# Where the block sums of the last batch's first weight matrix are made: group 1 early and by way of DRAM, group 0 at an earlier place in the plan

## The chip, the cores and the metric

The kernel runs as one program on one core of a Trainium2 chip. The metric is device time in microseconds (us). Before the change the median of three runs is 398.04 us (397.66 to 398.58). Profiles show one execution with the start and end of every instruction: PE is TensorE (PEld its weight loads), DVE is VectorE, ACT ScalarE, POOL GpSimd, SP the engine whose queue issues most DMAs.

## The reference, cut to what matters

```
for t in range(S):                                   # S = 768, 4 batches, 8 heads of 48
    cur   = einsum('bhd,bhe->bhde', u * k[t], v[t])
    y[t]  = einsum('bhd,bhde->bhe', r[t], state + cur)
    state = w * state + einsum('bhd,bhe->bhde', k[t], v[t])
x  = y.transpose(0, 2, 1, 3).reshape(B, S, 384)
u_ = x + (x^T @ U @ V)^T                             # mixes along the sequence, rank 32
out = u_ + relu(u_ @ w_ch1) @ w_ch2                  # 384 -> 1536 -> 384
```

All is float32; the kernel keeps that precision by splitting operands into a high and a low part and multiplying hi*hi, lo*hi and hi*lo.

## The kernel before, in words

Work goes batch by batch (four of them). Attention of a batch runs in six chunks of 128 steps, merged into the MLP of the batch before, so that TensorE always has matrix products of the MLP to go on with. At the end of a batch's attention `c_g` (L1214) sums x with U on TensorE, `c_u` (L1237) adds the low-rank mix to x, and for batches 2 and 3 `c_store`, `c_blocks` and `c_turn` (L1296 to L1325) carry the result through DRAM and turn it into the transposed operands `uTh` and `uTl`.

The MLP's first layer multiplies by W1 (12 column blocks, each held as `w1s`, hi and lo), the second by W2 (`w2s`). For batches 0 to 2 it is plain (`m_1`, `m_2`). In the last batch the first layer takes three column blocks at a time (a group, `NG` = 4 of them) and forms their 18 block products from 15 products of sums (`fifteen`, L1411): sums of blocks of u (`u_sums`, L1347, 11 of them, needed once) and sums of blocks of W1 (`w_sums`, L1380, 9 for each group). For one group `w_sums` issues three additions hi + lo of whole W1 blocks (L1388), 15 additions or subtractions of 128 x 128 blocks into a tile `ws` (L1400), and for each of three sets of three sums a copy on ACT to the hi part `wh` (L1404) and a subtraction to the lo part `wl` (L1405). L1388, L1400 and L1405 may go to either DVE or POOL.

In `fifteen` each product is three matmuls into a PSUM bank (names c and a letter in the profile; group 0 also borrows the banks tr and sc). The copies `keep` (L1432), the differences `less` (L1436), and in `out` the final additions (L1441, L1443), the relu to `hh` (L1445, ACT) and the low part `hl` (L1447, DVE) follow. The chains D and A use the ring of two banks tagged "mm", as do G, H and so on in the groups after the first. A new chain can start in a bank only when the last `out` that reads it is done.

The order of all instructions is written out by a list scheduler in the kernel, `Plan` (L48): each operation gets a key, the time at which it is wanted (`at`, L1717), and a guess of its duration. An engine takes the operation that can start first, and among those that can start at the same time the one of the lowest key. An operation that can go to POOL or DVE is marked as using the two engines' shared port ("lock"), and the plan never runs two of these at once. Tiles with a tag come from a ring of so many buffers and are handed out strictly in the order of the keys. The order on each engine is then fixed; on the chip each engine runs its list in order and waits for semaphores.

The keys that matter here are in us of the plan: the last batch's MLP begins at t = 315.95, its attention ends at `end` = 270.3. `w_sums(0)` has the key t - 20 = 295.95, groups 1, 2 and 3 have 313.35, 333.7 and 354.05. Rings: "xl" (4 buffers) holds `gf`, `ut` and later x5, x4 and one `hl`; "xh" (4) the blocks that come back from DRAM (`ub`), the raw sums of u and x3 to x0; "kT" (2) attention's transposed k and then `ws`; "ldr", "ldk", "ks" (2 each, called `W_TAGS` after) attention's loads and then `wh` and `wl` of one set; "dv" (2) attention's dv, then the third hi + lo sum `wr` of a group and the low part of the sum u20. The other two hi + lo sums are kept in the tiles `ub` and `tab` (attention's own, free after its last chunk).

The lines around the change:

```
US, WS, A3 = (16.0, 2.5), (20.0, 10.0), (0, 7.5)
...
for g in range(NG):
    at(t - WS[g > 0] + (7.4 + 20.35 * (g - 1) if g else 0), lambda g=g: w_sums(g))
for i, (f, m) in enumerate(last_units()):
    at(t - FIRST3[i] * PER if i < 3 else t, f)
    t += m * PER / 3 if i > 2 else 0
```

Of the kernel before, what the change touches and what calls it, by code (L numbers as in the profile page):

```python
# [9 lines left out]
F32 = mybir.dt.float32  # L10
# [314 lines left out]
def rwkv_moe(ctx: ExitStack, tc: tile.TileContext, r, k, v, w, u, U, V, w1, w2, out):  # L325
# [38 lines left out]
    def wbuf(shape, dt, tag, bufs, name):  # L364
        return Buf(work, shape, dt, tag, bufs, name)
# [14 lines left out]
    def f32(ap):  # L380
        return ap.bitcast(F32)
# [12 lines left out]
    def on_dve(n, fn, w_, r_, port=False, dk=0.0):  # L394
        return op("DVE", dve(n), lambda: fn(nc.vector), w_, r_, lock=port, dk=dk)

    def on_act(n, fn, w_, r_, times=1, dk=0.0):
        return op("ACT", times * (act(n) - 94) + 94, fn, w_, r_, dk=dk)

    def on_either(n, fn, w_, r_, dk=0.0, only=None):  # L400

        ways = [("POOL", pool(n), lambda: fn(nc.gpsimd), True), ("DVE", dve(n), lambda: fn(nc.vector), True)]
        return one_of(ways, w_, r_, only, dk)
# [907 lines left out]
    def c_turn(b, t, ct):  # L1311
# [10 lines left out]
        if last and (ct, t) in ((1, 1), (2, 0)):  # L1322
# [22 lines left out]
    NG = NFT // 3  # L1345

    def u_sums():  # L1347

# [28 lines left out]
                    ops_u[ct, t] = ([(lambda uh=uh, ct=ct: uh.t[:, ct, :]), (lambda ul=ul, ct=ct: ul.t[:, ct, :])], [(uh, ct), (ul, ct)])  # L1377
        return [lambda a_=a_: one(*a_) for a_ in U_SUMS] + [plain]

    def w_sums(g):  # L1380

        f0 = 3 * g
        raw = [(lambda: ub.t.rearrange("p h d -> p (h d)"), ub), (lambda: tab.t, tab)]
        third = wbuf([128, DM], F32, "dv", 2, f"wr_{g}")
        raw.append((lambda: third.t, third))
        for i, (ap, buf) in enumerate(raw):
            wt = W1[f0 + i]
            on_either(384, lambda e, ap=ap, wt=wt: e.tensor_tensor(ap(), f32(wt.t[:, 0]), f32(wt.t[:, 1]), ALU.add), [buf], [wt])  # L1388
        for s, tag in enumerate(("ldr", "ldk", "ks")):
            hi, lo = (wbuf([128, 3, 128], F32R, tag, 2, f"w{'hl'[k]}_{g}_{s}") for k in range(2))  # L1390
            sm = wbuf([128, 3, 128], F32, "kT", 2, f"ws_{g}_{s}")
            for j, (n, blocks, signs) in enumerate(W_SUMS[3 * s:3 * s + 3]):
                def block(x):
                    i, c = x
                    return (lambda: raw[i][0]()[:, c * 128:(c + 1) * 128]), raw[i][1]
                (acc, rb) = block(blocks[0])
                rd = [rb]
                for x, sg in zip(blocks[1:], signs):
                    fb, rb = block(x)
                    on_either(128, lambda e, acc=acc, fb=fb, sg=sg, sm=sm, j=j: e.tensor_tensor(  # L1400
                        sm.t[:, j], acc(), fb(), ALU.add if sg > 0 else ALU.subtract), [(sm, j)], rd + [rb])
                    acc, rd = (lambda sm=sm, j=j: sm.t[:, j]), []
                ops_w[g, n] = ([(lambda hi=hi, j=j: hi.t[:, j]), (lambda lo=lo, j=j: lo.t[:, j])], [hi, lo])
            on_act(384, lambda hi=hi, sm=sm: nc.scalar.copy(hi.t, sm.t), [hi], [sm])  # L1404
            on_either(384, lambda e, hi=hi, lo=lo, sm=sm: e.tensor_tensor(lo.t, sm.t, f32(hi.t), ALU.subtract), [lo], [hi, sm])  # L1405
        for i in range(3):
            wt = W1[f0 + i]
            for c in range(NCT):
                ops_w[g, (i, c)] = ([(lambda k=k, wt=wt, c=c: wt.t[:, k, c * 128:(c + 1) * 128]) for k in range(2)], [wt])

    def fifteen(g):  # L1411

        b, f0 = B - 1, 3 * g
        banks, kept = {}, {}
        early = {"G": "tr", "I": "sc", "K": "av", "H": "tr", "J": "sc"} if g == 0 else {}
        homes = {"x5": ("xl", NXS), "x4": ("xl", NXS), "x3": ("xh", NXS), "x2": ("xh", NXS), "x1": ("xh", NXS), "x0": ("xh", NXS)}

        def product(chain, w_, u_, first=False, last=False):
            if first:
                banks[chain] = bank(early.get(chain, "mm"), f"c{chain}_{g}")  # L1420
            pt = banks[chain]
            (wf, wb), (uf, ub_) = ops_w[g, w_], ops_u[u_]

            def go():
                for j, (kw, ku) in enumerate(((0, 0), (1, 0), (0, 1))):
                    whole(pt.t[:, :TB], lhsT=wf[kw](), rhs=uf[ku](), start=first and j == 0, stop=j == 2, skip_group_check=True)
            pe(3 * MM, go, [pt], wb + ub_)

        def keep(name, chain):
            pt = banks[chain]  # L1430
            to = kept[name] = wbuf([128, TB], F32, *homes.get(name, ("ldv", 3)), f"{name}_{g}")
            on_act(384, lambda: nc.scalar.copy(to.t, pt.t[:, :TB]), [to], [pt])  # L1432

        def less(name, a_, b_, o_=ALU.subtract):
            to, x, y = kept[name], kept[a_], kept[b_]
            on_either(384, lambda e: e.tensor_tensor(to.t, x.t, y.t, o_), [to], [v_ for v_ in (x, y) if v_ is not to])  # L1436

        def out(name, chain, t, i, minus=False):
            x, pt = kept[name], banks[chain]
            if minus:  # L1440
                on_dve(384, lambda e: e.tensor_tensor(x.t, x.t, pt.t[:, :TB], ALU.subtract), [x], [pt])  # L1441
            else:
                on_dve(384, lambda e: e.tensor_tensor(x.t, pt.t[:, :TB], x.t, ALU.add), [x], [pt])  # L1443
            hh = xbuf([128, TB], F32R, *(("x", NX) if i == 0 else ("hh", NH)), f"hh_{b}_{t}_{f0 + i}")
            on_act(384, lambda: nc.scalar.activation(hh.t, x.t, AF.Relu), [hh], [x])  # L1445
            hl = wbuf([128, TB], F32R, "xl", NXS, f"hl_{b}_{t}_{f0 + i}") if i == 0 else xbuf([128, TB], F32R, "hl", NH, f"hl_{b}_{t}_{f0 + i}")
            on_dve(384, lambda e: e.scalar_tensor_tensor(hl.t, x.t, 0.0, f32(hh.t), ALU.max, ALU.subtract), [hl], [x, hh])  # L1447
            hs[b, t, f0 + i] = (hh, hl)

        def s_G():  # L1450
            product("G", (0, 0), "u51", True)
            keep("x1", "G")

        def s_s32():
            product("G", "w193", (0, 1))
            keep("x5", "G")

        def s_H():
            product("H", (0, 1), "u40", True)
            keep("h", "H")  # L1460
            less("x1", "h", "x1")

        def s_I():
            product("I", (1, 0), "u15", True)
            keep("x2", "I")

        def s_s16():
            product("I", "w328", (0, 0))
            keep("x4", "I")

        def s_K():
            product("K", "w34", "u36", True)
            keep("x0", "K")

        def s_s8():
            product("K", "w26", "u12")
            keep("x3", "K")

        def s_J():
            less("x3", "x3", "h", ALU.add)  # L1480
            product("J", (1, 2), "u20", True)
            keep("j", "J")
            less("x2", "j", "x2")
            less("x0", "j", "x0")

        def s_D():
            product("D", (2, 1), "u10", True)
            keep("d", "D")
            less("x5", "x5", "d")

        def s_A():
            product("A", (2, 2), "u17", True)
            keep("a", "A")
            less("x4", "x4", "a")

        def s_E():
            product("D", "w136", "u14")
            out("x4", "D", 0, 2, True)

        def s_B():  # L1500
            product("A", "w257", "u49")
            out("x5", "A", 1, 2, True)

        def s_F():
            product("D", "w176", (1, 0))
            out("x3", "D", 1, 1)
            out("x2", "D", 0, 1)

        def s_C():
            product("A", "w262", (2, 1))  # L1510
            out("x1", "A", 1, 0)

        def s_s1():
            product("A", "w37", "u48")
            out("x0", "A", 0, 0)
        return dict(G=s_G, s32=s_s32, H=s_H, I=s_I, s16=s_s16, K=s_K, s8=s_s8, J=s_J, D=s_D, A=s_A, E=s_E, B=s_B, F=s_F, C=s_C, s1=s_s1)
# [212 lines left out]
    LATE_DG = 4  # L1729
    PWI, KD = 0.0, False  # L1730
    FIRST3 = 3.2, 2.5, 1.8
    US, WS, A3 = (16.0, 2.5), (20.0, 10.0), (0, 7.5)
    SC, SU_, TABLES = 2.0, 0.0, 60.0
    at(-101, lambda: ends.append(pe(214, fill, [wk], [])))

# [68 lines left out]
    for b in range(B):  # L1804
# [37 lines left out]
        if last:  # L1842
            for i, f in enumerate(u_sums()):
                at(end + US[0] + US[1] * i, f)
            for g in range(NG):
                at(t - WS[g > 0] + (7.4 + 20.35 * (g - 1) if g else 0), lambda g=g: w_sums(g))
            for i, (f, m) in enumerate(last_units()):
                at(t - FIRST3[i] * PER if i < 3 else t, f)
                t += m * PER / 3 if i > 2 else 0
            continue  # L1850
# [45 lines left out]
```

## Time and profile before

| what | us |
|---|---|
| median of three runs (range) | 398.04 (397.66 to 398.58) |
| the profiled execution | 398.01 |
| its span, first to last instruction | 396.3 |
| busy in it: PE / DVE / ACT / POOL | 388.0 / 320.8 / 156.2 / 110.1 |

Busy time of PE is of overlapping, pipelined matmuls, so gaps between the starts of matmuls tell more than it. A row of a timeline gives start, duration (of all the merged instructions together), engine, line, operation, out<-in, forms, count, and in brackets the idle time before it with what ended it. The letter p in the rows stands for a bank of the plain MLP products, ub in a DMA row for the blocks that come back from DRAM, ud for the place in DRAM where they wait.

### The profile page before, as it was taken

The numbers are of one execution on the slowest core, as the hardware profiler recorded it, in microseconds if no ns is written. First come the engines' busy times: TensorE is split into PE (matmuls) and PEld (weight loads), VectorE is DVE, ScalarE is ACT, GpSimd is POOL, SyncE is SP. The second block draws the span as 40 slices with busy tenths as digits, with TensorE's granted clock in tenths as the row PEclk, the third lists the DMA queues.
The fourth block names the chain that finished last, engine by engine and source line by source line (L and its number), as shares of the span: only waits on it lengthen the run. The fifth ranks groups of instructions, "written<-read, shape, count | busy, mean of one in ns | idle before, by whom it ended". The sixth has DMA issues, their size and how long they took to land.

```text
span 396.3 us, 11793 instructions
## 1 busy us (share of the span) xinstructions
PE 388.0 (98%) x4794; PEld 371.8 (94%) x4794; DVE 320.8 (81%) x739; ACT 156.2 (39%) x384; POOL 110.1 (28%) x165
## 2 busy tenths in 40 slices
PE   8999999999999999999999999999999998999995
PEld 7898999999899999999999999999999997999995
DVE  6899999998999848896794688979547889888463
ACT  3369658635651322010113201522213573554530
POOL 2982142531534024331010142631002236130000
PEclk9999999999999999999999999999999999999999
DMA  9979799698759885873787857900292010000003
GB/s 147 166 204 249 152 230 245 103 198 211 139 84 190 131 197 87 151 113 58 159 139 122 157 118 121 177 5 2 69 171 63 0 61 0 2 0 1 2 0 126
DMA packets 189852, 45.08 MB, mean 114 GB/s; under 512 B 174686, under 2 KB 188256, under 8 KB 189792
## 3 DMA queue, kind: packets, MB, share of 16 engines
q1 hardware_dynamic: 186240, 43.08, 56.0%
q10 hardware_dynamic: 3552, 1.18, 1.4%
q8 instruction: 39, 0.64, 0.7%
q14 instruction: 21, 0.17, 0.2%
HBM read 36.57 MB, written 7.67 MB: 112 GB/s over the span
## 4 chain that ended last, share of the span: by engine, by line
PE 84%; DVE 10%; DMA 2%; SPq 1%; issue 1%; ACT 1%; DVEq 0%; ACTq 0%
PE p L389 57%; PE pav L919 2%; PE pav L925 2%; PE bank_tr L389 2%; PE bank_sc L389 2%; PE bank_tr L1022 2%; PE pav L1071 2%; DVE hl L1447 1%; PE cA L389 1%; PE wake L389 1%; DMA raw_w<-in_moe_w_ch_dram 1%; SPq L775 1%; DVE x L1436 1%; PE cD L389 1%; PE bank_tr L899 1%
## 5 line engine op out<-in xcount | busy, mean ns | idle before, releaser
L389 PE MATMUL p<-uTh,w1s 128*128 128x384 f32 x432 | 112.0, 340 | 0.3 <-DVE hl L1534 0.3
L389 PE MATMUL p<-w2s,hh 128*128 128x384 f32 x528 | 111.4, 338 | 0.0
L389 PEld LDWEIGHTS p<-w2s,hh 128*128 128x128 f32 x528 | 92.6, 188 | 0.8
L1533 ACT ACTIVATE hh<-p 128x384 fp32r<-128x384 f32 x72 | 35.4, 492 | 139.7 <-PE p L389 127.3
L389 PEld LDWEIGHTS p<-uTh,w1s 128*128 128x128 f32 x432 | 76.9, 188 | 1.6 <-DVE hl L1534 0.6
L389 PE MATMUL p<-uTl,w1s 128*128 128x384 f32 x216 | 72.4, 335 | 0.0
L389 PE MATMUL p<-w2s,hl 128*128 128x384 f32 x264 | 62.6, 335 | 0.0
L1534 DVE SCALAR_TENSOR_TENSOR hl<-p,hh 128x384 fp32r<-128x384 f32 x72 | 39.8, 553 | 25.4 <-ACT hh L1533 24.5
L389 PEld LDWEIGHTS p<-w2s,hl 128*128 128x128 f32 x264 | 47.3, 188 | 0.0
L389 PEld LDWEIGHTS p<-uTl,w1s 128*128 128x128 f32 x216 | 40.5, 188 | 0.0
L785 POOL MEMSET ks<- 128x128 f32 x24 | 4.8, 206 | 62.6 <-PE bank_tr L899 62.6
L919 PEld LDWEIGHTS pav<-vsw,am 64*64 64x64 f32 x288 | 17.4, 134 | 4.5 <-issue 3.5
L919 PE MATMUL pav<-vsw,am 64*64 64x48 f32 x288 | 19.9, 221 | 0.0
L919 PE MATMUL pav<-ldv,am 64*64 64x48 f32 x288 | 19.5, 221 | 0.4 <-DVE x L1129 0.4
L795 POOL TENSOR_TENSOR dv<-ldr,ldk 128x384 f32<-128x384 f32 x15 | 15.3, 1022 | 14.7 <-DVE kT L824 4.5
L925 PE MATMUL pav<-S,rT 48*64 48x48 f32 x528 | 19.4, 218 | 0.0
L1445 ACT ACTIVATE hh<-x 128x384 fp32r<-128x384 f32 x24 | 12.0, 525 | 16.3 <-DVE x L1443 11.8
L1447 DVE SCALAR_TENSOR_TENSOR hl<-x,hh 128x384 fp32r<-128x384 f32 x24 | 15.5, 681 | 2.6 <-ACT hh L1445 2.4
L1325 POOL TENSOR_TENSOR uTl<-ut,uTh 128x384 fp32r<-128x384 f32 x4 | 4.1, 1015 | 48.6 <-ACT uTh L1324 25.5
L919 PEld LDWEIGHTS pav<-ldv,am 64*64 64x64 f32 x288 | 17.0, 134 | 0.5 <-issue 0.5
L925 PEld LDWEIGHTS pav<-S,rT 48*64 48x64 f32 x528 | 17.5, 135 | 0.0
L795 POOL TENSOR_TENSOR dv<-dv,ub 128x384 f32<-128x384 f32 x12 | 12.1, 1012 | 18.7 <-DVE w2s L659 8.9
(338 smaller groups left out, 825.5 us busy)
## 6 DMA issues: line engine op xcount, KB each, us to landing
raw_w<-in_moe_w_ch_dram SPq DMA_DIRECT2D x24, 384.0 KB, 4.7
out_dram<-x SPq DMA_DIRECT2D x21, 192.0 KB, 2.2
ldr<-in_r_dram SPq DMA_DIRECT2D x20, 192.0 KB, 4.1
ldk<-in_k_dram SPq DMA_DIRECT2D x20, 192.0 KB, 4.5
ldv<-in_v_dram SPq DMA_DIRECT2D x20, 192.0 KB, 4.6
bl<-in_r_dram SPq DMA_DIRECT2D x79, 48.0 KB, 3.0
bl<-in_k_dram SPq DMA_DIRECT2D x79, 48.0 KB, 2.4
ub<-ud SPq DMA_DIRECT2D x15, 192.0 KB, 3.0
```

The source lines that it names most:

```text
L389: return nc.tensor.matmul(*args, **kw)
L785: op("POOL", 250, lambda: nc.gpsimd.memset(ks.t[:, :, D:], 0.0), [(ks, "pad")], [])
L795: on_either(384, lambda e, a_=a_, b_=b_: e.tensor_mul(dv.t, a_()[:, :, :D], b_()[:, :, :D]), w_, r_, only="POOL" if front(n) else None)
L919: return nc.tensor.matmul(to(q, j, i), lhsT=am[j].t[half, q, :], rhs=vsw[n].t[half, q, :] if j else vt()[half, 2 * q, :], start=((alone or ...
L925: return nc.tensor.matmul(to(q, row, i), lhsT=rT.t[rows, q, i * C2:(i + 1) * C2], rhs=St[n, i].t[rows, q, :], start=False, stop=((alone or ...
L1022: return nc.tensor.matmul(abs_[n][j].t[:, q * C:(q + 1) * C], lhsT=kT.t[rows, q, :], rhs=rT.t[rows, q, :], start=True, stop=True)
L1071: return nc.tensor.matmul(avp[n][j].t[i * C2:(i + 1) * C2, q * D:(q + 1) * D], lhsT=ams[n][j].t[:, q, i * C2:(i + 1) * C2], rhs=vt()[:, 2 ...
L1325: on_either(384, lambda e: e.tensor_tensor(ul.t[:, ct, :], ut.t, f32(uh.t[:, ct, :]), ALU.subtract), [(ul, ct)], [ut, (uh, ct)])
L1445: on_act(384, lambda: nc.scalar.activation(hh.t, x.t, AF.Relu), [hh], [x])
L1447: on_dve(384, lambda e: e.scalar_tensor_tensor(hl.t, x.t, 0.0, f32(hh.t), ALU.max, ALU.subtract), [hl], [x, hh])
L1533: on_act(384, lambda: nc.scalar.activation(hh.t, pt.t[:, :TB], AF.Relu), [hh], [pt])
L1534: on_dve(384, lambda e: e.scalar_tensor_tensor(hl.t, pt.t[:, :TB], 0.0, f32(hh.t), ALU.max, ALU.subtract), [hl], [pt, hh])
```

## The change

For group 1 (`BY_DRAM`) `w_sums` is called with the key `end` - 6 = 264.3 instead of 313.35. Its three hi + lo sums go to three buffers of "xl", its `wh` and `wl` to "xh", and six DMAs store these to a tile `wd` in DRAM. At the old key (313.35) `w_load` fetches them with six DMAs into the buffers of "ldr", "ldk" and "ks", from which the products read them as before. Group 0's key goes from 295.95 to 279.95 (`WS[0]` from 20 to 36); groups 2 and 3 keep theirs. The sums are planned set by set instead of all three in one call, with the same key. The plain blocks of W1 are only entered into a table (`w_plain`), which issues nothing. In `out` the low part `hl` is now marked `port=True`: the plan counts it as a user of the port shared by DVE and POOL.

```
+    BY_DRAM = (1,)
+    W_TAGS = "ldr", "ldk", "ks"
...
-    def w_sums(g):
+    wd_pool = ctx.enter_context(tc.tile_pool(name="wd", bufs=1, space=bass.MemoryType.DRAM))
+    wd = {g: Buf(wd_pool, [3, 2, 128, 3, 128], F32, None, 1, f"wd{g}") for g in BY_DRAM}
+    w_raw = {}
+
+    def w_sums(g, s):
...
+        early = g in BY_DRAM
+        if g not in w_raw:
+            if early:
+                w_raw[g] = [(lambda t_=t_: t_.t, t_) for t_ in (wbuf([128, DM], F32, "xl", NXS, f"wr_{g}_{i}") for i in range(3))]
+            else:
+                third = wbuf([128, DM], F32, "dv", 2, f"wr_{g}")
+                w_raw[g] = [(lambda: ub.t.rearrange("p h d -> p (h d)"), ub), (lambda: tab.t, tab), (lambda: third.t, third)]
...
+        hi, lo = (wbuf([128, 3, 128], F32R, *(("xh", NXS) if early else (W_TAGS[s], 2)), f"w{'hl'[k]}_{g}_{s}") for k in range(2))
+        sm = wbuf([128, 3, 128], F32, "kT", 2, f"ws_{g}_{s}")
...
+        if early:
+            for k, t_ in enumerate((hi, lo)):
+                dma(lambda q, k=k, t_=t_: q.dma_start(wd[g].t[s, k], f32(t_.t)), [(wd[g], (s, k))], [t_], 128, 1536)
+
+    def w_load(g, s):
+
+        parts = [wbuf([128, 3, 128], F32R, W_TAGS[s], 2, f"w{'hl'[k]}_{g}_{s}") for k in range(2)]
+        for k in range(2):
+            dma(lambda q, k=k: q.dma_start(f32(parts[k].t), wd[g].t[s, k]), [parts[k]], [(wd[g], (s, k))], 128, 1536)
...
-            on_dve(384, lambda e: e.scalar_tensor_tensor(hl.t, x.t, 0.0, f32(hh.t), ALU.max, ALU.subtract), [hl], [x, hh])
+            on_dve(384, lambda e: e.scalar_tensor_tensor(hl.t, x.t, 0.0, f32(hh.t), ALU.max, ALU.subtract), [hl], [x, hh], port=True)
...
-    US, WS, A3 = (16.0, 2.5), (20.0, 10.0), (0, 7.5)
+    US, WS, A3, WM = (16.0, 2.5), (36.0, 10.0), (0, 7.5), -6.0
...
-                at(t - WS[g > 0] + (7.4 + 20.35 * (g - 1) if g else 0), lambda g=g: w_sums(g))
+                at(t - 50, lambda g=g: w_plain(g))
+                for s in range(3):
+                    at(t - WS[g > 0] + (7.4 + 20.35 * (g - 1) if g else 0), lambda g=g, s=s: (w_load if g in BY_DRAM else w_sums)(g, s))
+                    if g in BY_DRAM:
+                        at(end + WM, lambda g=g, s=s: w_sums(g, s))
```

## Rows read from the trace of the kernel before

**Rows 1.** The page: busy us of the engines, PE's busy tenths in 40 slices.
```profile
PE 388.0 (98%) x4794; PEld 371.8 (94%) x4794; DVE 320.8 (81%) x739; ACT 156.2 (39%) x384; POOL 110.1 (28%) x165
...
PE   8999999999999999999999999999999998999995
```

**Rows 2.** Stretches: busy us (and instructions) of PE, PEld, DVE, ACT, POOL; clock, DMA.
```profile
260.00:281.00 21.00, 21.00 (x282) 20.14 (x284) 16.12 (x47) 5.51 (x15) 4.14 (x6) 1.00 0.01 2
281.00:300.00 19.00, 19.00 (x152) 18.86 (x152) 9.87 (x19) 5.22 (x13) 0.82 (x1) 1.00 0.64 137
...
324.90:336.10 11.20, 9.60 (x50) 8.22 (x50) 11.20 (x20) 5.22 (x12) 7.08 (x8) 1.00 0.00 0
...
347.90:351.50 3.60, 3.22 (x19) 2.75 (x18) 3.60 (x8) 2.49 (x6) 2.07 (x5) 1.00 0.00 0
351.50:387.10 35.60, 35.60 (x206) 35.43 (x205) 22.73 (x51) 16.74 (x35) 0.65 (x1) 1.00 0.00 1
```

**Rows 3.** The chain that ended last: start, us, what.
```profile
287.60 28.60 PE p L389 x165
```

**Rows 4.** PE's timeline: batch 3's sum with U, then chains of groups 0 to 2.
```profile
280.95 1.20 PE L1190 MATMUL bank_tr<-x,Uf 128*32 128x96 f32 x48
...
321.60 0.33 PE L389 MATMUL bank_sc<-uTl,wh 128*128 128x384 f32 x1
...
322.29 0.51 PE L389 MATMUL cA<-uTh,w1s 128*128 128x384 f32 x2
...
332.78 0.43 PE L389 MATMUL cG<-uTh,wh 128*128 128x384 f32 x1
...
335.24 0.80 PE L389 MATMUL cH<-sum_u,w1s 128*128 128x384 f32 x3 [1.33 <-DVE x L1443]
...
348.65 0.79 PE L389 MATMUL cG<-sum_u,w1s 128*128 128x384 f32 x3 [0.38 <-DVE x L1443]
```

**Rows 5.** DVE's timeline from group 0's last differences on.
```profile
319.78 0.55 DVE L1371 TENSOR_TENSOR uTl<-raw_u,uTh 128x384 fp32r<-128x384 f32 x1
...
326.05 1.09 DVE L1405 TENSOR_TENSOR wl<-ws,wh 128x384 fp32r<-128x384 f32 x1
...
330.96 0.72 DVE L1405 TENSOR_TENSOR wl<-ws,wh 128x384 fp32r<-128x384 f32 x1
331.60 3.11 DVE L1447 SCALAR_TENSOR_TENSOR hl<-x,hh 128x384 fp32r<-128x384 f32 x3
334.64 0.55 DVE L1443 TENSOR_TENSOR x<-cA,x 128x384 f32<-128x384 f32 x1
...
381.01 1.49 DVE L1447 SCALAR_TENSOR_TENSOR hl<-x,hh 128x384 fp32r<-128x384 f32 x3
```

**Rows 6.** POOL's timeline: hi + lo sums of W1 (of groups 1 and 2).
```profile
275.21 1.01 POOL L1388 TENSOR_TENSOR ub<-w1s 128x384 f32<-128x384 f32 x1 [2.04 <-DVE tab L1388]
...
331.76 1.27 POOL L1388 TENSOR_TENSOR tab<-w1s 128x384 f32<-128x384 f32 x1 [0.49 <-DVE wl L1405]
332.98 1.32 POOL L1388 TENSOR_TENSOR wr<-w1s 128x384 f32<-128x384 f32 x1
```

**Rows 7.** DVE's timeline: group 0's sums begin; attention's last output; group 1's third.
```profile
270.60 0.49 DVE L1400 TENSOR_TENSOR ws<-ws,wr 128x128 f32<-128x128 f32 x2
...
275.63 0.64 DVE L1129 TENSOR_TENSOR x<-pav,x 64x192 f32<-64x192 f32 x2
...
316.41 0.55 DVE L1388 TENSOR_TENSOR wr<-w1s 128x384 f32<-128x384 f32 x1
```

**Rows 8.** SP's issues in the stretch of the change.
```profile
254.92 1.43 SPq L751 DMA_DIRECT2D vsw<-in_v_dram  x2
281.29 1.34 SPq L1579 DMA_DIRECT2D out_dram<-x  x3
...
292.25 1.61 SPq L1308 DMA_DIRECT2D ub<-ud  x3
```

**Rows 9.** DMA issues: count, KB each, median us from issue to landing.
```profile
ub<-ud SPq DMA_DIRECT2D x15, 192.0 KB, 3.0
```

More of the change, by code (lines that the diff above doesn't have):

```diff
@@ L1378, in u_sums @@
         return [lambda a_=a_: one(*a_) for a_ in U_SUMS] + [plain]
-    def w_sums(g):
+    wd_pool = ctx.enter_context(tc.tile_pool(name="wd", bufs=1, space=bass.MemoryType.DRAM))
+    wd = {g: Buf(wd_pool, [3, 2, 128, 3, 128], F32, None, 1, f"wd{g}") for g in BY_DRAM}
+    w_raw = {}
+    def w_sums(g, s):
         f0 = 3 * g
[L1383 to L1405, printed above, removed]
@@ new lines, in w_sums @@
+        early = g in BY_DRAM
[5 more added lines that the diff above has]
+                w_raw[g] = [(lambda: ub.t.rearrange("p h d -> p (h d)"), ub), (lambda: tab.t, tab), (lambda: third.t, third)]
+            for i, (ap, buf) in enumerate(w_raw[g]):
+                wt = W1[f0 + i]
+                on_either(384, lambda e, ap=ap, wt=wt: e.tensor_tensor(ap(), f32(wt.t[:, 0]), f32(wt.t[:, 1]), ALU.add), [buf], [wt])
@@ new lines, in w_sums, with block @@
+        raw = w_raw[g]
+        hi, lo = (wbuf([128, 3, 128], F32R, *(("xh", NXS) if early else (W_TAGS[s], 2)), f"w{'hl'[k]}_{g}_{s}") for k in range(2))
+        sm = wbuf([128, 3, 128], F32, "kT", 2, f"ws_{g}_{s}")
+        for j, (n, blocks, signs) in enumerate(W_SUMS[3 * s:3 * s + 3]):
+            def block(x):
+                i, c = x
+                return (lambda: raw[i][0]()[:, c * 128:(c + 1) * 128]), raw[i][1]
+            (acc, rb) = block(blocks[0])
+            rd = [rb]
+            for x, sg in zip(blocks[1:], signs):
+                fb, rb = block(x)
+                on_either(128, lambda e, acc=acc, fb=fb, sg=sg, j=j: e.tensor_tensor(
+                    sm.t[:, j], acc(), fb(), ALU.add if sg > 0 else ALU.subtract), [(sm, j)], rd + [rb])
+                acc, rd = (lambda j=j: sm.t[:, j]), []
+            if not early:
+                ops_w[g, n] = ([(lambda j=j: hi.t[:, j]), (lambda j=j: lo.t[:, j])], [hi, lo])
@@ new lines, in w_sums @@
+        on_act(384, lambda: nc.scalar.copy(hi.t, sm.t), [hi], [sm])
+        on_either(384, lambda e: e.tensor_tensor(lo.t, sm.t, f32(hi.t), ALU.subtract), [lo], [hi, sm])
+        if early:
[5 more added lines that the diff above has]
+            dma(lambda q, k=k: q.dma_start(f32(parts[k].t), wd[g].t[s, k]), [parts[k]], [(wd[g], (s, k))], 128, 1536)
+        for j, (n, _, _) in enumerate(W_SUMS[3 * s:3 * s + 3]):
+            ops_w[g, n] = ([lambda k=k, j=j: parts[k].t[:, j] for k in range(2)], parts)
@@ L1406, in w_sums, with w_plain @@
+    def w_plain(g):
         for i in range(3):
-            wt = W1[f0 + i]
+            wt = W1[3 * g + i]
             for c in range(NCT):
```

## The prediction, made before the changed kernel was run

> **What bounds the kernel now.** I read the page first: PE is busy for 388.0 of 396.3 us, and its slices are full except at the start, near 320 to 350 us and at the end [rows 1]. The granted clock is 1.00 in every stretch used below [rows 2]. So only gaps of PE can be won. A dense stretch of PE gives the price of one matmul: 165 of them in 28.60 us, 0.1733 us each [rows 3]. With it the table of stretches shows where matmuls are missing [rows 2]. From 324.9 to 336.1 there is room for 11.20 / 0.1733 = 64.6; 50 are counted, of which two were already under way when it began (one lasts about 0.34 us and the next starts 0.17 us behind it), so 48: 16.6 x 0.1733 = 2.9 us lost. From 347.9 to 351.5 there is room for 20.8, about 18 begin: 0.5 us lost. From 351.5 to 387.1 none is missing (206 in room for 205). What is lost is thus 3.4 us, all in the last batch's groups 0 and 1.
>
> The timeline of PE names the waits: H of group 1 stands 1.33 us and G of group 2 0.38 us for a DVE addition x (L1443) that frees their bank [rows 4]; the rest of the 2.9 us is many short gaps of 0.1 to 0.3 us between the same two moments. The timeline of DVE shows why that addition is late [rows 5]. From 326.05 to the end of the x at 334.64 + 0.55 = 335.2 DVE never rests: it is busy 11.20 of 11.20 us in the stretch [rows 2]. In it stand two `wl` of group 1, which the next products need much later, and three `hl` that take 3.11 us where three later ones take 1.49; meanwhile POOL runs two hi + lo sums of group 2, from 331.76 to 334.30 [rows 6]. Group 1's sums have a lower key (313.35) than group 0's last outputs, so the plan lets them go first.
>
> **The change, part by part.**
>
> *Group 1's sums leave the stretch 316 to 332.* These are the third hi + lo sum (L1388, at 316.41 [rows 7]), 15 block sums, three ACT copies and three `wl`. What matters is the time in front of the late x at 334.64: without the two `wl` (about 1.0 and 0.64 us) and with everything else at its undisturbed pace, five `hl` and six additions or differences (two and five of these stand between the rows shown) at about 1.49 / 3 = 0.5 us each, the DVE needs 11 x 0.5 = 5.5 us where it took 335.2 - 326.05 = 9.1 [rows 5]. That is x done by 331.6, or earlier, since the first `wl` of the group, before 324, goes too. H of group 1 wants its bank 1.33 us before 335.24, at 333.9 [rows 4]; since PE also loses its short gaps before that (2.9 - 1.3 = 1.6 us), it will want it at about 332.3. So the wait is gone with 0.7 us to spare. What may take the place of `wl`: group 2's sums, which no longer wait for `ub` and `tab` and have only the third sum and, with two buffers of `ws`, the first two sets (9 of 15 block sums) open to them at that time. That is 0.5 + 9 x 0.25 = 2.7 us by [rows 7], but from 316 on, and with key 333.7 behind group 0's outputs. Gain 2.9 us; bounds: 1.6 us if H waits as long as now, 2.9 us as all that is lost there.
>
> *Group 2's hi + lo sums move too.* `ub` and `tab` are free as soon as group 0's sums are made, so two of the three can run from about 285 on, where DVE is busy for 9.87 of 19.00 us [rows 2]. This takes the two POOL sums away from beside the `hl` [rows 6]. It is part of the 2.9 us. Group 1's own outputs then have fewer sums before them; of the 0.5 us at 347.9 to 351.5 I count half, 0.25 us (bounds 0 and 0.5).
>
> *What is put into 258 to 285.* Here three hi + lo sums, 15 block sums and three `wl`: 3 x 0.5 + 15 x 0.25 + 3 x 0.5 = 6.8 us if all on DVE; two of group 1's hi + lo sums, tab and ub, stood there before at 274.5 and 275.21 [rows 6], so some 5.8 us more. DVE is idle for 4.9 us of 260 to 281 and for 9.1 us of 281 to 300, POOL for 16.9 and 18.2 [rows 2]: it fits. Cover on PE: the sum with U at 280.95 waits for attention's last output, done at 275.63 + 0.64 = 276.3 [rows 4, 7]. PE comes to it only by its key, behind the MLP's work of batch 2, so attention may be 4.7 us later before the sum with U is late. Behind that, the last sum of u for chain A is done at 319.78 + 0.55 = 320.3 and used at 322.29 [rows 4, 5], another 2.0 us. Cost 0; if both covers were used up, each further us of delay costs one.
>
> *The rings and SP.* The `wh` and `wl` of group 1 take six buffers of "xh" in turn, ahead of the six loads `ub` of batch 3; `wr` takes three of four in "xl", ahead of `gf`. The six stores go to SP between its last attention load, issued by 254.92 + 1.43 = 256.4, and 281.29, where it issues nothing [rows 8]. A load of this size lands in 3.0 us [rows 9], and I take the same for a store; the third set waits for the first stores, some 3 us. The first `ub` load is at 292.25 [rows 8], about 12 us behind. Cost 0. On the way back the six loads wait on SP until group 0's products have freed the buffers: the first pair when the last product with the first set's sums ends, at 321.60 + 0.33 = 321.9 [rows 4], so it is landed by 321.9 + 2 x 0.5 + 3.0 = 325.9. It is needed at 332.78 less what PE gains, 331: 5 us to spare. Behind them in SP's queue stand only the last stores of batch 2 and, some 60 us later, outputs. Cost 0; without the cover the price would be the lateness itself.
>
> *The low part `hl` marked as a port user.* Its own arithmetic is unchanged. The plan now keeps POOL from a sum while an `hl` runs, and the other way round. On the chip the two hardly ran side by side before: three `hl` and two POOL sums took 3.11 us together; in a row they would take 1.49 + 2 x 1.01 = 3.5 [rows 5, 6]. So the mark loses up to 0.4 us where such a pair meets and saves the plan from an order that doesn't hold. I take -0.3 us for all groups (bounds 0.4 us gained, 1.2 us lost, once for each of three groups).
>
> The Trainium skill ("SBUF — State Buffer", section "SBUF: two separate sides") says that the port pair shared by the two engines is an exclusive lock, held for a whole instruction, the other engine standing still. By that rule the mark costs nothing, and the sum would be 0.3 us better. The rows above agree nearly, but 3.1 us is less than the 3.5 of a strict turn; I keep the 0.3.
>
> Sum: 2.9 + 0.25 - 0.3 = 2.85 us less. The profiled execution took 398.01 us, 1.7 more than its span and within 0.03 of the median, so the sum is made against 398.0: **395.2 us**.
>
> **The rivals.** (1) *Half of it.* The plan places group 2's sums in front of group 0's last outputs after all, because an idle engine takes what is ready without regard to the key: the x at 334.64 comes forward only by the two `wl` and H still waits about 1 us, or the wait returns at group 1's outputs. Left: 1.4 us of gain, 396.6. For it: groups 1 to 3 leave DVE full at 347.9 to 351.5 now (3.60 of 3.60 [rows 2]). Against: DVE needs 5.5 us where 7 are there.
>
> (2) *No change.* The sums for group 1 come out no earlier than needed, as a ring that is handed out in order holds them (`ws` waits for attention's two buffers of "kT"), or the chain of waits simply moves to the next gap. 398.0. For it: group 0's first `ws` ran only at 270.60 [rows 7], late in the idle time that I count on. Against: what held it was its third sum, in "dv", which group 1 no longer uses.
>
> (3) *Slower: the lock.* With `hl` locked, each of the six `hl` of groups 1 to 3 can stand behind a POOL sum of 1.01 us [rows 6] in the outputs that free chain A's bank. From the point where these outputs have less than 1 us to spare, which is so for groups 1 and 2 if DVE stays as full as it is at 347.9, PE waits two to three sums for each of them: 2 x 2.5 = 5 us lost against 2.9 gained, 400.1. Against: after 351.5 PE lost nothing with the same outputs, and DVE is busy only for 22.73 of 35.60 us there.
>
> **How the numbers follow.** Forecast (394.4 to 396.0) 0.55; half, 0.18; no change, 0.13; slower, 0.10; the remaining 0.04 is more gain than all I count, below 394.4. What a measurement can tell from no change is 0.2%, 0.8 us, so 397.2 and 398.8 are the limits. Faster takes the forecast, the gain beyond it, and nearly all of the half (0.17): 0.76. Same: 0.13 and what is left of the half, 0.14. Slower: 0.10. The range to 8 in 10 goes from 394.2 to 397.6, which are also the bounds of the terms (2.9 + 0.5 + 0.4 = 3.8 us of gain at one end, 1.6 - 1.2 = 0.4 at the other): it holds the forecast, the half and the nearer part of no change (0.06), 0.79 in all.
>
> **What would show it.** Right: some 60 or more matmuls in the 11.2 us that begin with group 0's C, no wait of PE for x (L1443) over 0.3 us in groups 0 and 1; no `wl` on DVE between 316 and 332; the `hl` of group 0 near 0.5 us each; L1388 for group 2 on DVE or POOL before 300 but for the third; six more SP issues before 281 and six from 320 to 333; the sum with U still behind the same matmuls of batch 2. Wrong: PE waiting for `wh` or `wl` from DRAM in groups 0 and 1, for a raw sum of u in group 0, or a new wait for x in groups 1 to 3.

## The result, and the profile after

The changed kernel takes 393.53 us (median of 4 runs, 393.43 to 393.95) beside 398.31 us for the kernel before in the same job (4 runs, 397.66 to 399.32): ratio 0.988, 95% interval 0.9857 to 0.9903. The forecast of faster came true, but 393.53 lies below the range (394.2 to 397.6): the kernel gained more than was counted. Of all runs reported below, one of extra_load (400.02 us) is left out, as it fell in the chip's slower state.

The page after: PE's busy line, its slices, and the chain that ended last by engine.

```profile
PE 386.1 (99%) x4794; PEld 372.3 (95%) x4794; DVE 318.0 (81%) x740; ACT 157.0 (40%) x388; POOL 104.2 (27%) x164
...
PE   8999999999999999999999999999999999999995
...
PE 99%; DVE 0%; issue 0%
```

Beside [rows 1], the 8 among the 9s near 340 us is gone, and the chain is PE for 99% of its length. The stretches of the last batch after (columns as in [rows 2]):

```profile
260.00:281.00 21.00, 21.00 (x320) 20.00 (x319) 19.85 (x56) 7.18 (x20) 7.72 (x14) 1.00 0.17 60
...
324.00:336.00 12.00, 12.00 (x70) 11.82 (x69) 8.27 (x18) 7.52 (x17) 0.00 (x0) 1.00 0.22 66
...
348.00:352.00 4.00, 4.00 (x25) 3.94 (x24) 1.87 (x8) 2.26 (x5) 0.00 (x0) 1.00 0.00 0
```

Between 324 and 336 there is room for 12.00 / 0.1733 = 69.2 matmuls, and 70 stand there; DVE, which had no rest in [rows 2], is busy for 8.27 of 12.00 us; POOL, busy for 7.08 of 11.20 before, does nothing. The work went to 260 to 281, where DVE is now nearly full (19.85 of 21.00) and PE lost nothing. The timeline of PE after, then DVE's, then SP's:

```profile
279.67 1.20 PE L1190 MATMUL bank_tr<-x,Uf 128*32 128x96 f32 x48
...
314.77 0.68 PE L389 MATMUL bank_tr<-sum_u,w1s 128*128 128x384 f32 x3
...
330.06 0.33 PE L389 MATMUL cG<-uTh,wh 128*128 128x384 f32 x1
...
330.93 0.68 PE L389 MATMUL cH<-sum_u,w1s 128*128 128x384 f32 x3
...
343.86 0.68 PE L389 MATMUL cG<-sum_u,w1s 128*128 128x384 f32 x3
```

```profile
274.02 0.63 DVE L1129 TENSOR_TENSOR x<-pav,x 64x192 f32<-64x192 f32 x2
...
324.80 1.02 DVE L1471 SCALAR_TENSOR_TENSOR hl<-x,hh 128x384 fp32r<-128x384 f32 x2
...
328.54 1.48 DVE L1471 SCALAR_TENSOR_TENSOR hl<-x,hh 128x384 fp32r<-128x384 f32 x3
329.94 0.55 DVE L1467 TENSOR_TENSOR x<-cA,x 128x384 f32<-128x384 f32 x1
```

```profile
265.25 0.35 SPq L1419 DMA_DIRECT2D wd<-wh  x1
...
272.33 0.32 SPq L1419 DMA_DIRECT2D wd<-wl  x1
280.01 1.30 SPq L1603 DMA_DIRECT2D out_dram<-x  x3
...
321.02 0.38 SPq L1425 DMA_DIRECT2D wh<-wd  x1
321.50 0.41 SPq L1425 DMA_DIRECT2D wl<-wd  x1
```

H of group 1 and G of group 2 start without a wait (no bracket behind their rows; the waits of [rows 4] were 1.33 and 0.38 us), since the three `hl` take 1.48 us where they took 3.11 [rows 5] and the x behind them is done at 330.5.

**Two parts of the difference.** Up to 253 us both kernels have the same instructions in the same order on every engine, and PE keeps its order into group 0's products. I count from the first of these (`bank_tr<-sum_u`, 314.77 after) to the end of the span and call it the last stage. It lasts 391.7 - 314.77 = 76.93 us after, and 396.3 - 316.05 = 80.25 before: 3.3 us less. The other 1.3 us of the profiled pair arose before the change begins. It shows in these stretches, of before and then of after:

```profile
90.00:100.00 10.00, 10.00 (x205) 9.45 (x203) 8.66 (x21) 5.99 (x15) 2.23 (x3) 1.00 0.89 212
100.00:110.00 10.00, 9.61 (x249) 9.16 (x241) 9.81 (x26) 5.82 (x17) 4.80 (x6) 1.00 0.73 140
110.00:120.00 10.00, 10.00 (x118) 9.53 (x115) 9.93 (x26) 4.83 (x14) 3.39 (x5) 1.00 0.56 83
120.00:130.00 10.00, 9.70 (x84) 9.13 (x86) 9.23 (x21) 1.48 (x3) 4.56 (x4) 1.00 1.01 207
```

```profile
90.00:100.00 10.00, 10.00 (x205) 9.45 (x205) 9.88 (x25) 7.37 (x18) 2.68 (x4) 1.00 0.98 247
100.00:110.00 10.00, 10.00 (x258) 9.64 (x250) 9.81 (x26) 5.02 (x15) 4.29 (x5) 1.00 0.68 106
110.00:120.00 10.00, 10.00 (x117) 9.66 (x116) 9.92 (x25) 4.27 (x14) 3.40 (x5) 1.00 0.61 98
120.00:130.00 10.00, 10.00 (x102) 9.59 (x101) 9.38 (x21) 2.14 (x6) 4.64 (x4) 1.00 1.07 206
```

Read DVE's column first: 8.66 against 9.88 us in 90 to 100, 1.2 us lost, and then it has little rest in either kernel, so in this execution the loss is not caught up; PE pays behind it, at 100 to 110 (9.61) and 120 to 130 (9.70). What DVE stood for, for 1.27 us, is a relu on ACT that waits in ACT's queue behind a block of W (raw_w), and this block came late: SP issued it at 89.09 us, after at 86.94, and ACT's timeline has it some 5.3 us later in both, before and then after:

```profile
94.42 0.56 ACT L616 ACTIVATE raw_w<-raw_w 128x384 int32<-128x384 uint8 x1 [3.09 <-DMA raw_w<-in_moe_w_ch_dram]
```

```profile
92.30 0.55 ACT L616 ACTIVATE raw_w<-raw_w 128x384 int32<-128x384 uint8 x1 [0.88 <-DMA raw_w<-in_moe_w_ch_dram]
```

Row by row, PE's matmuls of before are 0.7 us behind those of after by 120 us and 1.3 by 130. The second step is another load: at 122 DVE waits 0.70 us for a block of attention's k (ldk), and PE 0.30 us for the `hl` behind it. raw_w thus explains a little over half of the 1.3 us.

### The profile page after: what moved, and what is told of

Read it like the earlier page. It is cut to its first block, busy times and chain, and to the rows that moved or that the text cites. A ratio compares the mean times of both kernels' runs of the same rounds, so it can differ in the third digit from the quotient of the medians.

```text
span 391.7 us, 11823 instructions
## 1 busy us (share of the span) xinstructions
PE 386.1 (99%) x4794; PEld 372.3 (95%) x4794; DVE 318.0 (81%) x740; ACT 157.0 (40%) x388; POOL 104.2 (27%) x164
## 4 chain that ended last, share of the span: by engine, by line
PE 99%; DVE 0%; issue 0%
PE p L389 66%; PE pav L919 3%; PE pav L925 3%; PE bank_sc L389 3%; PE bank_tr L389 3%; PE cA L389 2%; PE wake L389 2%; PE pav L1071 2%; PE cD L389 2%; PE bank_tr L1022 2%; PE bank_tr L899 1%; PE cK L389 1%; PE bank_tr L885 1%; PE ptr L835 1%; PE bank_tr L1190 1%; PE ptk L835 1%
## 5 line engine op out<-in xcount | busy, mean ns | idle before, releaser
L1598 DVE TENSOR_TENSOR x<-p,x 128x384 f32<-128x384 f32 x28 | 14.1, 548 | 2.9 <-PE p L389 2.8
```

Of the source, the lines that this page charges most:

```text
L1598: on_dve(384, lambda e, x=x, pt=pt: e.tensor_tensor(x.t, pt.t[:, :DM], x.t, ALU.add), [x], [pt], dk=XD if b == B - 1 and t == 0 else 0.0)
```

## The experiments

The question is what the 3.3 us are made of and where the 1.3 us come from. In the expectations, A says that the loss was `wl` standing ahead of `hl` and x in DVE's queue; B says that GpSimd's sums running beside the `hl` were the larger part; E1 says that the early loss differs from execution to execution whatever the kernel. The last stage of each profile, and the times:

| kernel | median, us (range, runs) | ratio to before (interval) | last stage, us |
|---|---|---|---|
| before, profiled | 398.31 (397.66 to 399.32, 4) | 1 | 80.25 |
| before_again | 397.06 (396.56 to 399.65, 12) | 0.9987 (0.9968 to 1.0006) | 80.2 |
| after, profiled | 393.53 (393.43 to 393.95, 4) | 0.988 (0.9857 to 0.9903) | 76.93 |
| after_again | 393.56 (393.37 to 398.0, 6) | 0.9893 (0.9862 to 0.9923) | 76.99 |
| after_third | 394.08 (393.38 to 395.05, 6) | 0.9912 (0.9882 to 0.9941) | 76.95 |
| port_only | 395.35 (394.1 to 398.9, 12) | 0.9948 (0.9923 to 0.9973) | 77.72 |
| mark_g0 | 395.96 (394.76 to 397.81, 12) | 0.9959 (0.9938 to 0.9981) | 78.44 |
| dram_only | 395.93 (394.82 to 396.69, 12) | 0.9955 (0.9936 to 0.9973) | 78.47 |
| sums_dve | 396.16 (394.72 to 396.99, 12) | 0.9953 (0.9928 to 0.9979) | 78.41 |
| pool_back | 395.74 (395.01 to 399.6, 12) | 0.9973 (0.9943 to 1.0002) | 78.74 |
| extra_load | 396.24 (394.06 to 399.23, 11) | 0.9967 (0.9935 to 0.9999) | 76.83 |
| lead15 | 395.23 (394.6 to 400.01, 12) | 0.9943 (0.9916 to 0.9971) | 76.93 |
| lead9 | 404.83 (403.91 to 407.01, 6) | 1.02 (1.016 to 1.024) | 77.05 |

The ratios are to the kernel before run in the same job (4 runs for the row after, else 23 or 29, medians 397.42 to 397.69, fastest 396.5 to 396.6); they weigh all runs and are not quotients of the medians. The last stage is free of what came before it, the fastest run nearly so, and they agree: before 396.5, after 393.37 (3.1 less), port_only 394.1 (2.4), dram_only 394.82 (1.7).

**port_only: the mark alone.**

```
 kernel before, in out():
-            on_dve(384, ... [hl], [x, hh])
+            on_dve(384, ... [hl], [x, hh], port=True)
```

> The kernel before with the mark alone: hl in the last batch counts as a user of the shared port; nothing else is changed. Theory A (the sums' place is what counts, the mark is an aid): H of group 1 still waits for x, about 1 us, and PE gets back at most 1 us: 397.3 to 398.3. Rival B (the three hl that ran beside two POOL sums were the cause, so the mark suffices): the 1.3 us wait is gone and most of the short gaps with it: 395.5 to 396.5.

PE's wait for H of group 1 is gone with all the `wl` still there; G waits 0.28 us. DVE's three `hl`, and POOL's two sums now on either side of them:

```profile
331.04 1.62 DVE L1447 SCALAR_TENSOR_TENSOR hl<-x,hh 128x384 fp32r<-128x384 f32 x3
332.58 0.55 DVE L1443 TENSOR_TENSOR x<-cA,x 128x384 f32<-128x384 f32 x1
```

```profile
330.29 1.02 POOL L1388 TENSOR_TENSOR tab<-w1s 128x384 f32<-128x384 f32 x1
332.80 1.01 POOL L1388 TENSOR_TENSOR ub<-w1s 128x384 f32<-128x384 f32 x1 [1.50 <-DVE hl L1447]
```

The last stage is 2.5 us shorter, and the median lies just below what B expected. The mark, which the prediction priced at a loss of 0.3, alone brings three quarters of the whole gain.

**dram_only: everything but the mark.**

```
 changed kernel, in out():
-            on_dve(384, ... [hl], [x, hh], port=True)
+            on_dve(384, ... [hl], [x, hh])
```

> The changed kernel without the mark on hl: group 1's sums early and by way of DRAM, group 0's key moved. Theory A: nearly all of the gain stays, 393.4 to 394.3, no wait of PE over 0.3 us in groups 0 and 1. Rival B: the hl run beside POOL sums again and a wait of about 1 us comes back: 394.7 to 396.5.

The last stage is 1.8 us shorter and the time is B's, though the waits are less than B's 1 us. The `wl` are out of the way, and what is left is two waits for G, 0.19 and 0.54 us. DVE where the first arises (both `hl`, then the second by itself), and POOL:

```profile
325.26 1.84 DVE L1471 SCALAR_TENSOR_TENSOR hl<-x,hh 128x384 fp32r<-128x384 f32 x2
...
325.73 1.37 DVE L1471 SCALAR_TENSOR_TENSOR hl<-x,hh 128x384 fp32r<-128x384 f32 x1
```

```profile
325.42 1.27 POOL L1460 TENSOR_TENSOR x<-x,h 128x384 f32<-128x384 f32 x1 [4.52 <-DVE x L1460]
```

Two `hl` take 1.84 us beside one addition on POOL; the same two take 1.02 after. It is the second that pays: it takes 1.37 us instead of 0.55 and ends at 327.10, 0.41 us behind the addition (325.42 + 1.27 = 326.69). The plan fills the POOL that the sums left with another addition, unless the mark forbids it. 2.5 and 1.8 are more than 3.3: the two edits in part take away the same waits.

**before_again and after_again: which key does what.** The first is the changed code without DRAM and without mark, group 0's key moved; the second is the changed kernel with group 0's key put back.

```
 before_again:  BY_DRAM = ()          after_again:  WS[0] = 20.0 (36.0 after)
```

> The changed kernel without the way by DRAM and without the mark; only group 0's key is at its new place. The order of all instructions on all five engines is then that of the kernel before, so it is the kernel before once more: 398.0 to 398.6. It is run for its own profile: a load of W blocks landed at 94.4 us in the kernel before and at 92.3 in the changed one, and DVE waited 1.3 us for it. Theory E1 (chance of an execution): the landing at 92 to 95 us varies and the times of this kernel spread by 1 us or more. Rival E2 (it goes with the program): here it lands late again, and PE has lost about 1.3 us by 130 us.

> The changed kernel with group 0's key at its old place, 20 before the MLP instead of 36; the order of all instructions on all five engines is then that of the changed kernel, so group 0's key is shown to do nothing by itself: 393.4 to 394.0. Theory E1: of its executions some are 1 us longer, as the load of W blocks near 92 us lands late. Rival E2: none is, and its profile shows the load in time.

Each has its partner's instructions in its partner's order on every engine: moving group 0's key does nothing. They are thus second looks at the same programs, and their last stages repeat to 0.1 us. The early part doesn't: in before_again the raw_w landed at 92.74 and group 0 began at 314.99 (316.05 before); in the profiled execution of after_again (398.0 us) it landed at 96.20 and group 0 began at 319.31. That is E1: the loss comes and goes with no change of order. Not all of the 4.5 us between 314.77 and 319.31 is raw_w's: PE is 2.5 us behind after by 130 us and loses the other 2.0 between 250 and 265, where DVE waits 1.14 us for a block of attention's k and PE 1.36 us for attention's x.

```profile
96.20 0.58 ACT L616 ACTIVATE raw_w<-raw_w 128x384 int32<-128x384 uint8 x1 [3.88 <-DMA raw_w<-in_moe_w_ch_dram]
```

**after_third: the changed kernel once more.**

> The changed kernel once more, beside pool_back of the same job, and to settle whether its early part is better by program or by chance. So far, counted from group 0's first product to the end of the span, the last stage lasted 76.93 and 76.99 us in two profiles of the changed kernel and 80.25 and 80.2 in two of the order of before; the part ahead of it, in which both have the same instructions in the same order, ended between 314.77 and 319.31. Theory 1 (early part by chance): last stage 76.9 to 77.1; the fastest run of it 393.4, as before, and its runs spread upward as those of before do, about half of them more than 0.75 above the fastest, median 393.8 to 395.0, ratio 0.990 to 0.993. Theory 2 (the changed program itself makes the early part better): nine of ten runs within 0.75 of the fastest, median 393.4 to 393.7, ratio 0.988 to 0.990.

Three of its six runs are within 0.3 of 393.38, three 1.1 to 1.7 above; median and ratio lie between the two theories' figures, nearer to chance. Over the three jobs 12 of 16 runs of the changed order are within 0.75 of its fastest, and 30 of 85 of the kernel before; but before_again, in the order of before, had 9 of 12, and dram_only, with the same loads in the early part as the changed kernel, 3 of 12. Whether the changed program has better odds there stays open; that the early part varies with no change of order is shown.

The profile of after_third also shows what a late block may cost: raw_w came 1.4 us later than in after, and yet group 0 began at 314.75, as early as there. DVE, 0.6 us behind at 100, had made it up by 131, and PE lost nothing.

```profile
93.68 0.59 ACT L616 ACTIVATE raw_w<-raw_w 128x384 int32<-128x384 uint8 x1 [2.25 <-DMA raw_w<-in_moe_w_ch_dram]
```

**pool_back: twelve useless additions on GpSimd beside group 0's `hl`.** PE, DVE, ACT and SP keep every instruction in its order. The cut shortens the operands: hh half k stands for 112 partitions of 192 columns.

```
 changed kernel, in out(), behind hl:
+            if g == 0:
+                spare = tabT.t.rearrange("p n c -> p (n c)")[:, :TB // 2]
+                for k in range(2):
+                    op("POOL", 1, lambda k=k: nc.gpsimd.tensor_tensor(spare, hh half k, hh half k, ALU.add), [tabT], [hh])
```

> The changed kernel with twelve useless additions on GpSimd, two of 112x192 at each of group 0's six hl (they read the hh that the hl reads, and write a table that nobody reads any more); PE, DVE, ACT and SP keep every instruction in its order, and GpSimd has nothing else between 320.4 and 339.7 us. Theory B (GpSimd's additions beside the hl lengthen them, and that is what the mark takes away): the five or six hl of 326 to 332 us, now 0.5 each, go to 0.8 to 1.05, x behind them comes 1 to 2 us later, PE waits again for x L1467 in front of cG or cH, 0.3 to 1.5 us, and the last stage lasts 77.4 to 79.0 instead of 76.95: 393.9 to 395.5 us. Theory A (the loss of before was wl's turn in DVE's queue alone; GpSimd beside an hl costs nothing that PE sees): hl stay at 0.5, no wait of PE, last stage 76.9 to 77.1, the time of after_third within 0.3.

DVE's rows, POOL's, and PE's two waits:

```profile
324.99 1.33 DVE L1471 SCALAR_TENSOR_TENSOR hl<-x,hh 128x384 fp32r<-128x384 f32 x2
...
327.03 1.64 DVE L1460 TENSOR_TENSOR x<-j,x 128x384 f32<-128x384 f32 x2
...
329.98 2.33 DVE L1471 SCALAR_TENSOR_TENSOR hl<-x,hh 128x384 fp32r<-128x384 f32 x3
332.24 0.55 DVE L1467 TENSOR_TENSOR x<-cA,x 128x384 f32<-128x384 f32 x1
```

```profile
324.98 3.27 POOL L1475 TENSOR_TENSOR tabT<-hh 112x192 f32<-112x192 f32 x4 [4.35 <-ACT hh L1469]
329.83 5.58 POOL L1475 TENSOR_TENSOR tabT<-hh 112x192 f32<-112x192 f32 x8 [1.58 <-ACT hh L1469]
```

```profile
329.65 0.79 PE L389 MATMUL cG<-sum_u,w1s 128*128 128x384 f32 x3 [0.98 <-DVE x L1467]
332.84 0.79 PE L389 MATMUL cH<-sum_u,w1s 128*128 128x384 f32 x3 [0.29 <-DVE x L1467]
```

Three `hl` go from 1.48 to 2.33 us, the waits for x are back, 60 matmuls stand in 324 to 336 instead of 70 (1.7 us), and the last stage is 1.8 us longer; the median is 1.7 us above after_third's of the same job. Nothing else differs, so the cause that B names is shown: additions on GpSimd beside the `hl` cost PE time through the x behind them. That they were the larger part of the loss of before is not measured by this run, which puts more additions there than before had; port_only, where the `wl` stay and 2.5 of the 3.3 us come back, speaks for it, but there DVE's order changes too. Nor does any run move the `wl` and leave POOL's additions where they were, so the part of the `wl` by themselves stays open.

**mark_g0: the mark on group 0's `hl` only.** In port_only, `port=g == 0` for `port=True`.

> The kernel before with the mark on the hl of group 0 alone. Its matmuls have the same order as in port_only, on DVE and GpSimd only some sums behind 336 us stand otherwise. Theory: the mark's whole gain lies at group 0's outputs, where before lost the most: last stage 77.7 to 78.0 as in port_only (77.72), time 395.0 to 395.9, ratio 0.993 to 0.996. Rival: the mark earns at groups 1 to 3 too (0.5 us and more at 347.9 to 351.5): last stage 78.2 to 78.8, 395.7 to 396.6.

78.44: the rival is right. Group 0's outputs bring 1.8 of the 2.5 us; G of group 2 waits again, behind two `hl` of group 1 that run beside two sums on POOL. DVE's row, then PE's:

```profile
343.14 1.83 DVE L1447 SCALAR_TENSOR_TENSOR hl<-x,hh 128x384 fp32r<-128x384 f32 x2
```

```profile
345.96 0.79 PE L389 MATMUL cG<-sum_u,w1s 128*128 128x384 f32 x3 [0.42 <-DVE x L1443]
```

**sums_dve: the kernel before with all of w_sums' additions on DVE.**

```
 kernel before, the three on_either(...) in w_sums:
+    only="DVE"
```

> The kernel before with every sum of W1 blocks of the last stage on VectorE (23 instructions leave GpSimd; no mark, nothing by DRAM). Theory B (GpSimd's sums beside the hl were the larger part of the loss): though VectorE has more to do, the hl at 326 to 336 us take 0.5 each, the wait of PE for x in front of cH falls from 1.3 to under 0.5, and the last stage lasts 77.5 to 79.0 instead of 80.2: 394.7 to 396.2 us. Theory A (VectorE's own queue was too full, wl in front of hl and x): with more in that queue the waits for x stay or grow, last stage 80.0 to 82.0, 397.0 to 399 us.

78.41, 1.8 us less, though DVE has 22 instructions more. H and G no longer wait; two new waits stand earlier, cA's for x and bank_tr's for an `hl`. DVE's row, then PE's:

```profile
330.44 1.48 DVE L1447 SCALAR_TENSOR_TENSOR hl<-x,hh 128x384 fp32r<-128x384 f32 x3
```

```profile
325.37 0.45 PE L389 MATMUL cA<-uTh,wh 128*128 128x384 f32 x1 [0.55 <-DVE x L1441]
...
328.23 0.44 PE L389 MATMUL bank_tr<-w2s,hl 128*128 128x384 f32 x1 [0.49 <-DVE hl L1447]
```

A alone can't explain that a fuller DVE is earlier; the order of its queue differs too, so this run supports B; the cost itself is shown by pool_back.

**extra_load: two useless loads of 1024 packets of 16 bytes, at 52 us.** Nothing else moves.

```
 changed kernel, among the loads (spare is a new small tile):
+    def more(k):
+        sv = bass.AP(..., ap=[[64, 128], [8, 8], [1, 4]])
+        op("SP", 1, lambda: nc.sync.dma_start(spare.t[:, k], sv), [(spare, k)], [landing[8][1]])
+    at(60.0, lambda: [more(k) for k in range(2)])
```

> The changed kernel with two useless DMAs of 1024 packets of 16 bytes each, issued by SP among the loads of 50 to 60 us; every other instruction of every engine keeps its order. Theory (the early part's time is set by the DMA engines, which are full over the first 70 to 85 us, so that whatever slows them there by a few us comes out at the end): 16 loads of 384 packets took some 11 us there, 0.11 us for 64 packets, so 2048 packets are worth up to 3.6 us; the raw_w that came between 92.3 and 96.2 comes 1.5 to 4 us later than 92.3, group 0's first product at 316 to 318.5 or later, and the fastest run is 1 to 3.6 above the 393.4 of the changed kernel: 394.4 to 397.0. The last stage keeps 76.9 to 77.1. Rival (the DMA engines have slack; the early loss is something else): fastest run 393.4 to 393.8.

The median is 2.2 us above after_third's (same chip, the job before), the fastest run 0.7 (less than the 1 to 3.6 expected), the last stage stays (76.83). In the profiled execution the raw_w comes at 97.32:

```profile
97.32 0.59 ACT L617 ACTIVATE raw_w<-raw_w 128x384 int32<-128x384 uint8 x1 [3.61 <-DMA raw_w<-in_moe_w_ch_dram]
```

So in this profile traffic put into the DMA queue at 52 us comes out at 97, and in most runs at the end: that queue can set the early part, though some runs absorb most of it.

**lead15 and lead9: the W loads wanted 3 us earlier or later, for a version that beats both.** `LEAD` 15.0 and 9.0 for 12.0.

> The changed kernel with the W blocks' loads wanted 3 us earlier (LEAD 15 for 12), so that the order of SP's loads changes from the first batches on. Does the early loss go? If the late load (raw_w landing between 92.3 and 96.2 us in the profiles, with DVE waiting for it) is late because it is asked for too late: the wait of ACT L616 there goes, group 0's first product comes at 314.5 to 314.8 in any run, the median is 393.2 to 393.6 and the spread shrinks. If it is late because the DMA engines are full until then (their share stands at 9 tenths over the first 70 to 85 us, SP's own issues stretch), an earlier request only takes the place of other loads: the same spread, or loads of attention late, 394 to 397 us.

> The changed kernel with the W blocks' loads wanted 3 us later (LEAD 9 for 12; the opposite of lead15, which gave 394.6 at the fastest and 395.23 at the median). If the full DMA engines are the limit of the early part, less competition for attention's loads there may give a steadier early part: fastest 393.2 to 393.6, median 393.4 to 393.9. If the W loads are what is late, they come later still: 394.5 to 397. The last stage should stay at 76.9 to 77.3.

Neither does. Earlier loads give 394.6 at the fastest, 1.2 above the changed kernel, and no narrower spread; later ones 403.9, some 7 us above the most that was expected. There PE falls 10.4 us behind the changed kernel between 73 and 88 us. 7.7 us of it are four waits, the longest of 3.4 and 2.0 us for converted W1 blocks; the rest goes with the granted clock, which was 1.00 up to 75 us, 0.64 from 75 to 80, where the wait of 3.4 us begins, and 0.50, the lower of its two levels (1.2 for 2.4 GHz), from 80 to 85; from 90 on it was 1.00 again.

```profile
80.00:85.00 5.00, 2.19 (x6) 1.79 (x7) 4.83 (x11) 3.56 (x8) 0.00 (x0) 0.50 1.20 207
```

The last stage is the same in both (76.93, 77.05).

## Why the prediction was wrong

*"What is lost is thus 3.4 us, all in the last batch's groups 0 and 1."* The 3.4 us are right: 3.3 were recovered. "All" is what failed. The profiled execution of before had lost another 1.3 us before 130 us, under slices that show a 9 for anything from 90% up; the stretches I tabulated began at 260. Two rows of the page that I passed over, the chain of before by engine and by line, named it:

```profile
PE 84%; DVE 10%; DMA 2%; SPq 1%; issue 1%; ACT 1%; DVEq 0%; ACTq 0%
PE p L389 57%; PE pav L919 2%; PE pav L925 2%; PE bank_tr L389 2%; PE bank_sc L389 2%; PE bank_tr L1022 2%; PE pav L1071 2%; DVE hl L1447 1%; PE cA L389 1%; PE wake L389 1%; DMA raw_w<-in_moe_w_ch_dram 1%; SPq L775 1%; DVE x L1436 1%; PE cD L389 1%; PE bank_tr L899 1%
```

raw_w has 1% of the chain and SP's queue another, some 4 us each, and no product of the last batch's groups waited for a DMA. In before_again, where little was lost early, raw_w isn't in the chain. The baseline of 398.0, taken from three runs, is in the upper half of the 85 of all jobs (median 397.58, fastest 396.49), and the four runs of the changed kernel were all near its fastest. Against medians over all jobs, 397.58 and 393.64 (16 runs), the gain is 3.9 us, of which 3.3 are the change's and 0.6 the early part's. The change's 3.3 us alone, taken from 398.0, would have given 394.7, inside the range: what carried the result out of it is the early part, which as far as is shown is luck of the executions, and which the sum held at nothing.

*-0.3 us for the mark.* The sign was wrong. On top of everything else it gains 78.47 - 76.93 = 1.5 us, alone 2.5. I priced only what a strict turn costs a pair that meets; what counts is that the plan, believing that an addition on POOL costs an `hl` nothing, places additions beside the `hl`, and that PE waits for the x behind the `hl`, not for POOL's sum.

*2.9 + 0.25 us for the moved sums.* Too much for them alone: 1.8 us (dram_only), since POOL's other additions move in beside the `hl`. With the mark the same place loses nothing: x was done at 330.5 (forecast: by 331.6; the execution after was 1.3 us earlier when the stage began), and G of group 2 waits no more, so of the 0.5 us at 347.9 to 351.5 all came back, not half. So 1.8 + 1.5 = 3.3 took the place of 3.15 - 0.3 = 2.85: two errors of opposite sign, in a place rightly found.

*The covers held.* Attention's last output was done at 274.65 for a sum with U at 279.67, 5.0 us of slack where 4.7 were worked out. The stores went out from 265.25 to 272.65, between SP's attention loads and its next issue at 280.01. The first loads were issued by 321.91 (forecast: from 321.9) for a use at 330.06, without a wait on PE; that one group can wait in DRAM at no cost is as forecast.

*The rivals.* Half: what dram_only does (1.8 of 3.3), but the mark keeps the changed kernel from it. No change and the lock's loss: not seen; a marked `hl` stands behind no addition that PE could notice.

*The Trainium skill's rule* ("SBUF — State Buffer", section "SBUF: two separate sides") pointed the right way, and its condition decides here: it counts a DVE instruction with two SBUF inputs among those that take the shared pair, but only against a GpSimd one that reads SBUF. In pool_back `hl` and x<-j,x, which read two tiles in SBUF, are slowed by 0.15 to 0.3 us each on average, and x<-cA,x, which reads one from a PSUM bank, takes 0.55 as always beside POOL's additions. The rule's "fully blocks" fits the single rows too: the second `hl` of dram_only, and the second and third of the three in [rows 5], which take 1.37 and 1.35 us, each end 0.41 us behind the end of the addition beside them. What was too dear in the prediction is a turn counted as the sum of undisturbed durations, 3.5 us for those three and two additions where 3.11 were measured: behind the addition an `hl` needs 0.41 us more and not its 0.5. In pool_back it is the same: three `hl` and about three additions, whose shortest of twelve took 0.51 us, would make 1.48 + 3 x 0.51 = 3.0 us and took 2.33; the additions were lengthened as well, to 0.70 each (eight in 5.58).

## What to carry to other kernels

Before a loss is called local, tabulate the whole span in short stretches for each engine, look in the chain for what isn't the bounding engine, and ask whether another execution of the same program would lose there too; a stage's length, counted from a row that both kernels have, is free of what came before. A mark that changes only what the plan believes is priced by where it makes the plan put the work, not by the instruction's own time. Two edits that remove the same wait don't add: run each alone.

## What was not expected of the hardware

One GpSimd addition of 128x384 can make a DVE instruction that reads two tiles in SBUF last 1.37 us instead of 0.55 (dram_only, and the kernel before), while merged rows, such as two in 1.84 us, make it look like a mild slowing of each. And with the same order of instructions, SP's issue of one W load came anywhere from 86.94 to 91.09 us and its landing from 92.30 to 96.20 (after and after_again), with the end 4.6 us apart (spans 391.7 and 396.3), 2.5 us of it lost by 130 us and 2.0 behind a later load of k: in a kernel whose PE is busy for 99% of the time, the loads are the unsteady part. What makes SP late there in one execution and not in another isn't settled.
